# First pair of an attention and rational-MLP kernel: order of its loads, transposes and splits, and the matmul order of four MLP units

## The chip, the cores and the metric

The kernel runs on one core of one Trainium2 chip. The metric is the device time of one execution in microseconds (us); the figure for a kernel is the median of several executions. The profile is one further execution, taken by the hardware profiler; its times count from the first instruction (the span's start). Engines: PE is TensorE (matmuls; PEld are its weight loads), ACT is ScalarE, DVE is VectorE, POOL is GpSimd, SP is SyncE, which here only issues transfers. A name with q (SPq, ACTq) is the engine's queue of instructions, where transfers are issued.

## The reference

All inputs are float32 after the draw. There are 4 batches of 12 heads, 448 positions and 64 dimensions a head, then an MLP over 1792 tokens with 768 inputs and 2048 hidden units:

```
scores = (q @ k.T) / sqrt(64)
scores = cap * tanh(scores / cap)
attn   = softmax(scores)            # exp(scores - max) / (sum + 1e-9)
x      = heads side by side of (attn @ v)
h = x @ w_in
P = a[0] + a[1]*h + a[2]*h*h + a[3]*h*h*h
Q = 1 + |b[0]|*|h| + |b[1]|*h*h
out = (P / (Q + 1e-6)) @ w_out
```

## The kernel before, in words

**Attention** goes by pairs of heads p = 0 to 23. K and Q of a pair are transposed on PE (`prep_k`: three transposes of 128 columns and one of K's last 64 positions for both heads; `prep_q`: four of 112), and each is split into a high part in the matmul's number format and a low rest: kh (L350), kl (L351), qh (L378 on ACT for pair 0, L381 on DVE for the others), ql (L384). A tile (p, n) is 128 keys of pair p against its 448 queries: six matmuls (L429), kl·qh, kh·ql and kh·qh for each of two heads, into one of three PSUM buffers ps of two banks; tile (p, 3) of an odd pair holds the 64 leftover keys of two pairs in twelve matmuls. ACT takes the tile by tanh (L440) and, with cap as scale, exp (L457). DVE adds up the exps of tiles 0, 1 and 2 (L463). PE multiplies them by V (L511, L528) and sums (L594, L556).

**Order.** `Plan` keeps a list of operations with estimated costs and due times and writes out, at build time, one fixed order for every engine; on the chip each engine works its list strictly in that order and waits on semaphores. `past` gives the plan the time at which a load of the first ring is taken to have landed. `visits(p)` says in which order a pair's steps are handed to the plan; for pair 0 it is tile 0, tile 1, transposes and splits of pair 1, tile 2, and four idle matmuls (`fill`, L405), which write zeros into the first ps buffer to keep PE working. `busy` (L398) does the same around the first transposes, by the counts in WARM2.

**First loads.** Ahead of the branch on cap (the bounded body runs when |cap| is at most 40, as here) the first four heads are loaded by twelve transfers. I name them by head: K0 to K3 (384 positions, 96 KB each), T0 to T3 (K's last 64 positions, 16 KB each), Q0 to Q3 (112 KB each). Pair 0 needs heads 0 and 1, pair 1 heads 2 and 3. Before, SP issues K0, K1, T0, then K2, K3, T2, T3, Q2, Q3, and ACT issues cap (to all 128 partitions), T1, Q0, Q1. The transfers of the two queues SP and ACT use eight semaphores (DMAHW0 to 7 in the order below) in turn, so the ninth transfer is issued only when the one that had its semaphore first has landed, and what is behind it in its queue waits as well. After six warm matmuls (L1292) every engine reads cap, branches, and begins the body; `preload_act_table_set` loads the table for tanh and exp (L655).

**PSUM.** prep of pairs 0 and 1 uses the banks mi (K) and pv (Q), of pair 2 mi, and of pair 3 both banks of the third ps buffer (ps_129 in the order before, ps_133 in the order of the change). So tile (2, 2), which is written there, waits until DVE has read pair 3's transposes.

**MLP.** A unit is 128 hidden units for 896 tokens: stage1 is 36 matmuls for h into a ps buffer, of 512 and of 384 tokens (two banks); `rational` takes it through ACT and DVE (L889 to L902); `stage2` (L928) multiplies by w_out, and L955 empties its PSUM. The first four units run by L858, six matmuls for each of six input blocks, alternating between the two banks; all later units run by L843, in two blocks of 18, one a bank.

Of the kernel before, what the change touches and what calls it, by code (L numbers as in the profile page):

```python
# [13 lines left out]
I32 = mybir.dt.int32  # L14
# [32 lines left out]
WARM2 = (2, 1, 3)  # L47
# [25 lines left out]
class Plan:  # L73
# [7 lines left out]
    def __init__(self):  # L81
        self.ops = []
        self.wr, self.rd = {}, {}
        self.n = 0
        self.free = [4500.0, 4600.0, 3700.0, 3700.0, 9900.0]
        self.dma_free = 11000.0
        self.where, self.over = {}, {}
# [160 lines left out]
class Body:  # L248
# [82 lines left out]

    def prep_k(self, p):
# [61 lines left out]
    def busy(self, p, n):  # L394

        z = self.io["arena_r"][:, 0:512]
        for _ in range(WARM2[n] if p == 0 else 0):
            self.op(PE, 213, lambda: self.nc.tensor.matmul(self.PS[2][:, 1], z[:, 0:128], z, start=True, stop=True),  # L398
                    [], [("ps", 2), "turn"])
# [15 lines left out]
    def scores(self, p, n):  # L415
# [16 lines left out]
        self.op(PE, SC_NS * len(sets) + TURN_NS * first, run, [k for name, _ in sets for k in K(name)], w, early=E_SC)  # L432
# [208 lines left out]
    def attention(self):  # L641
# [11 lines left out]
        self.prep_k(0)  # L653
        self.prep_q(0)
        self.op(ACT, 1290, lambda: nc.scalar.preload_act_table_set("exp_and_others"), [], ["table"])  # L655
# [19 lines left out]
        def visits(p):  # L675
# [10 lines left out]
            if p == 0:  # L686
                return [s0, s1, (k, 1), (q, 1), s2, (self.fill, FILL[0])]
# [137 lines left out]
    def stage1(self, u, between=None):  # L825
# [384 lines left out]
    def run(self):  # L1210
        tc = self.tc
        self.rslot, self.made, self.later = {}, set(), {}
        with ExitStack() as ctx:
# [31 lines left out]
def attention_rational_mlp(ctx: ExitStack, tc: tile.TileContext, q, k, v, cap, moe_w_in, moe_w_out,  # L1245
# [4 lines left out]
    with tc.manual_schedule():  # L1250
# [15 lines left out]
        nc.scalar.dma_start(acap, cap.partition_broadcast(128))  # L1266
# [13 lines left out]
        nc.gpsimd.dma_start(a, moe_a.partition_broadcast(128))  # L1280
        nc.vector.tensor_scalar(acap.bitcast(I32), acap.bitcast(I32), 0x7FFFFFFF, None, ALU.bitwise_and)
# [11 lines left out]
        rv = nc.values_load(acap.bitcast(I32)[0:1, 0:1])  # L1293
# [40 lines left out]
```

## Time and profile before

| what | us |
|---|---|
| median of 3 runs (lowest, highest) | 659.59 (659.20, 659.76) |
| the profiled execution, its own time | 659.91 |
| its span, first to last instruction | 657.9 |
| PE busy in the span | 647.8 (98%) |
| DVE busy | 541.9 (82%) |
| ACT busy | 442.2 (67%) |

Busy shares are means over stages with different limits: attention runs to about 181 us, the MLP from there to the end. A row of the timeline gives start, duration, engine, line, operation, out<-in, shapes and count; the brackets give the idle time just ahead of it and what ended it. Neighbouring instructions of one kind are merged into a row.

### The profile page before, as it was taken

How to read it: one execution, taken by the hardware profiler on the slowest of the kernel's cores; microseconds unless marked ns; L12 is line 12 of the kernel's file. 1: busy time of each engine (PE TensorE's matmuls, PEld its weight loads, DVE VectorE, ACT ScalarE, POOL GpSimd, SP SyncE). 2: the span in 40 equal slices, each digit the busy share in tenths (PEclk: the TensorE clock that was granted, in tenths of full speed). 3: DMA queues.
4: the chain of work that ended last, by engine and by line, in shares of the span. 5: the costliest groups of instructions: out<-in, count | busy, mean ns of one | idle time of the engine just before them, and what ended most of it. 6: DMA issues, size and time to landing. Idle time of an engine off the chain costs nothing.

```text
span 657.9 us, 9767 instructions
## 1 busy us (share of the span) xinstructions
PE 647.8 (98%) x3820; PEld 542.0 (82%) x3820; DVE 541.9 (82%) x662; ACT 442.2 (67%) x531; POOL 85.0 (13%) x141
## 2 busy tenths in 40 slices
PE   8999999999999999999999999999999999999996
PEld 5555555655478899999999999999999999999996
DVE  4789899899679987977987897899699789969653
ACT  5899999999857867875457466646646565663560
POOL 4013222321200000020012002101200210120030
PEclk9999999999999999999999999999999999999999
DMA  7757864943230332195158118614821671481086
GB/s 170 186 138 171 203 163 100 199 119 85 59 86 22 128 141 92 51 197 113 48 106 158 49 49 152 158 43 86 166 68 49 128 142 60 95 170 33 1 139 203
DMA packets 79095, 74.45 MB, mean 113 GB/s; under 512 B 48456, under 2 KB 67264, under 8 KB 79040
## 3 DMA queue, kind: packets, MB, share of 16 engines
q1 hardware_dynamic: 68240, 48.68, 25.7%
q0 software_dynamic: 9648, 24.80, 22.5%
q8 instruction: 32, 0.52, 0.3%
q10 hardware_dynamic: 1152, 0.25, 0.2%
q14 instruction: 23, 0.19, 0.1%
HBM read 47.98 MB, written 25.65 MB: 112 GB/s over the span
## 4 chain that ended last, share of the span: by engine, by line
PE 82%; DVE 6%; ACT 4%; DMA 3%; issue 3%; POOL 0%; SPq 0%; DVEq 0%; POOLq 0%; ACTq 0%
PE ps L843 31%; PE ps L928 17%; PE mi L928 9%; PE pv L928 9%; PE ps L429 6%; PE mi L511 3%; DMA arena_r<-dn 2%; ACT etiles L440 2%; PE mi L594 1%; PE pv L511 1%; ACT etiles L457 1%; PE pv L528 1%; PE ps L343 1%; DMA dn<-arena_f 1%; PE ps L366 1%
## 5 line engine op out<-in xcount | busy, mean ns | idle before, releaser
L843 PE MATMUL ps<-arena_r,ring 128*128 128x512 f32 (+1 forms) x924 | 207.6, 363 | 0.0
L843 PEld LDWEIGHTS ps<-arena_r,ring 128*128 128x128 f32 x924 | 167.7, 188 | 17.5
L295 POOL DMA_DIRECT2D out_dram<-arena_f x49 | 42.0, 863 | 423.6 <-ACT arena_f L955 423.6
L928 PE MATMUL ps<-arena_r,etiles 128*128 128x384 f32 x462 | 89.7, 335 | 0.6 <-ACT arena_f L955 0.5
L457 ACT ACTIVATE etiles<-etiles,acap 128x896 f32<-128x896 f32 x84 | 85.5, 1053 | 0.2
L440 ACT ACTIVATE etiles<-ps 128x896 f32<-128x896 f32 x84 | 74.7, 921 | 13.9 <-PE ps L429 13.7
L928 PEld LDWEIGHTS ps<-arena_r,etiles 128*128 128x128 f32 x462 | 80.8, 188 | 1.3 <-ACT arena_f L955 0.8
L928 PE MATMUL mi<-arena_r,etiles 128*128 128x384 f32 x231 | 77.2, 336 | 0.0
L928 PE MATMUL pv<-arena_r,etiles 128*128 128x384 f32 x231 | 77.0, 335 | 0.0
L429 PEld LDWEIGHTS ps<-arena_r 64*128 64x128 f32 x576 | 51.0, 184 | 25.2 <-ACT etiles L457 7.8
L889 ACT ACTIVATE arena_f<-ps,b 128x896 f32<-128x896 f32 x32 | 32.3, 1009 | 54.8 <-PE ps L843 54.7
L429 PE MATMUL ps<-arena_r 64*128 64x448 f32 x576 | 67.7, 376 | 1.2 <-DVE arena_r L384 0.9
L789 ACT ACTIVATE arena_f<-arena_f 128x768 f32<-128x768 f32 x32 | 29.4, 918 | 44.1 <-DMA arena_f<-in_moe_w_out_dram 31.0
L901 ACT CAST etiles<-arena_f 128x896 fp32r<-128x896 f32 x32 | 30.3, 946 | 42.0 <-DVE arena_f L900 42.0
L893 DVE SCALAR_TENSOR_TENSOR arena_f<-arena_f,bab 128x896 f32<-128x896 f32 x32 | 36.8, 1150 | 23.8 <-ACT arena_f L890 23.8
L898 DVE SCALAR_TENSOR_TENSOR arena_f<-arena_f,one 128x896 f32<-128x896 f32 x32 | 36.7, 1148 | 11.3 <-ACT arena_f L896 11.3
L928 PEld LDWEIGHTS pv<-arena_r,etiles 128*128 128x128 f32 x231 | 43.3, 188 | 0.6
L928 PEld LDWEIGHTS mi<-arena_r,etiles 128*128 128x128 f32 x231 | 43.3, 188 | 0.6
L928 PE MATMUL ps<-ring,etiles 128*128 128x384 f32 x210 | 42.0, 334 | 0.0
L902 DVE TENSOR_TENSOR etiles<-arena_f,etiles 128x896 fp32r<-128x896 f32 x32 | 34.9, 1089 | 7.0 <-ACT etiles L901 6.8
L891 ACT ACTIVATE arena_f<-ps,a 128x896 f32<-128x896 f32 x32 | 35.3, 1104 | 3.5 <-DVE arena_f L899 3.5
L897 DVE SCALAR_TENSOR_TENSOR arena_f<-arena_f,a,ps 128x896 f32<-128x896 f32 x32 | 36.6, 1144 | 0.4
(145 smaller groups left out, 1124.2 us busy)
## 6 DMA issues: line engine op xcount, KB each, us to landing
out_dram<-arena_f POOLq DMA_DIRECT2D x49, 384.0 KB, 6.2
arena_f<-in_moe_w_out_dram SPq DMA_DIRECT2D x16, 768.0 KB, 4.3
arena_f<-in_moe_w_in_dram SPq DMA_DIRECT2D x16, 768.0 KB, 4.8
out_dram<-arena_f SPq DMA_DIRECT2D x13, 384.0 KB, 2.5
ring<-in_q_dram SPq DMA_DIRECT2D x44, 112.0 KB, 3.6
arena_r<-dn POOLq DMA_DIRECT2D x20, 224.0 KB, 5.3
ring<-in_k_dram SPq DMA_DIRECT2D x33, 128.0 KB, 3.1
ring<-in_v_dram SPq DMA_DIRECT2D x11, 384.0 KB, 3.7
```

The lines of the kernel that those rows point to most:

```text
L295: self.op(eng, (625 if local else 450) if eng == SP else 1050, lambda: e.dma_start(out, in_, **accum), r, w, nbytes=nbytes, **kw)
L429: m = nc.tensor.matmul(self.PS[i][:, j, 0:448], st[r], mv[r], start=y == 0, stop=y == len(ops) - 1)
L440: self.op(ACT, act_ns(896, True), lambda: nc.scalar.activation(e, ps, AF.Tanh), pk + ["table"], [ek], early=E_TANH)
L457: self.op(ACT, act_ns(size, sk[0][0] == "ps", 1), lambda: nc.scalar.activation(e, src, AF.Exp, scale=acap), sk + ["table"], [ek])
L843: r = nc.tensor.matmul(po[:, ts], w[:, y, kc], mv, start=kc == 0 and z == 0, stop=kc == KC - 1 and z == 2)
L889: self.op(ACT, act_ns(n, True, 1), lambda: T.activation(Bt, h, AF.Abs, scale=b[:, 0:1]), hk, bk)
L891: self.op(ACT, act_ns(n, True, 2), lambda: T.activation(A, h, AF.Identity, scale=a[:, 3:4], bias=a[:, 2:3]), hk, ak)
L893: self.op(DVE, dve_ns(n, 1), lambda: stt(Bt, C, bab[:, 1:2], Bt, ALU.mult, ALU.add), ck + ["bab"], bk)
L897: self.op(DVE, dve_ns(n, 1), lambda: stt(A, A, a[:, 1:2], h, ALU.add, ALU.mult), hk, ak)
L898: self.op(DVE, dve_ns(n, 1), lambda: stt(Bt, Bt, one, C, ALU.add, ALU.mult), ck, bk)
L902: self.op(DVE, dve_ns(n), lambda: V.tensor_tensor(GL(), A, f32(GH()), ALU.subtract), ak + K("gh", ig), K("gl", ig))
L928: r = nc.tensor.matmul(po[n][:, 0:384], st, mv[:, 384 * n:384 * n + 384], start=(y == 0 and x == 0), stop=(y == self.NCH - 1 and x == 2))
```

## The change

What it does, in the order of the program:

- cap is loaded twice: one number by ACT's queue (cap1), which decides the branch, and the 128-partition copy by POOL's queue, from which c1 and the exp's scale come.
- The twelve loads are dealt out anew: SP issues Q0, K0, T0, T1, K2, K3, T2, T3; ACT issues cap1, Q1, K1, Q2, Q3, and then loads the table, ahead of the branch.
- `prep_first` replaces prep for pair 0: Q is transposed first, into pv, then K into the third ps buffer; qh and ql are made in two halves of 224 queries, kh and kl for the first 128 keys and then for the other 384. Two `busy` matmuls (L398) are left of six.
- Tile (0, 0) runs in the order kh·qh, kh·ql, kl·qh. Pair 0 is handed to the plan as tile 0, transposes and splits of pair 1, tile 1, tile 2.
- The plan's assumed landing times and engine start times are changed.
- In the four L858 units each six matmuls go as three into one bank and three into the other.

```diff
-WARM2 = (2, 1, 3)
+WARM2 = (1, 1, 3)
...
-        self.free = [4500.0, 4600.0, 3700.0, 3700.0, 9900.0]
+        self.free = [4300.0, 4200.0, 3700.0, 3700.0, 9900.0]
...
+    def prep_first(self):
+        nc = self.nc
+        idn, c1 = self.c["ident"], self.c["c1"]
+        raw = self.io["ring"][ring_of(0)]
+        name, (S, QL) = self.qset(0)
+        K = lambda s: (name, s)
+        (pk, bk), (pq, bq) = (self.PS[2][:, 0], ("ps", 2)), (self.PV, "pv")
...
+        self.busy(0, 0)
+        self.op(PE, 390, tq, rq, [bq, "turn"])
+        self.op(PE, 440, tk, rk[:3], [bk, "turn"])
+        self.op(PE, 110, lambda: nc.tensor.transpose(pk[:, 384:512], raw["kt"][:, 0], idn), rk[3:], [bk + ("2",), "turn"])
+        self.busy(0, 1)
+        for x, s in enumerate(("qh", "qh2")):
+            t = slice(224 * x, 224 * x + 224)
+            self.op(ACT, act_ns(224, True, 1),
+                    lambda t=t: nc.scalar.activation(S[:, 2, t], pq[:, t], AF.Identity, scale=c1), [bq], [K(s)], early=E_PR)
...
+        high(slice(0, 128), "")
+        for x, s in enumerate(("", "2")):
+            t = slice(224 * x, 224 * x + 224)
+            self.op(DVE, dve_ns(224, 1),
+                    lambda t=t: nc.vector.scalar_tensor_tensor(QL[:, t], pq[:, t], c1, f32(S[:, 2, t]), ALU.mult, ALU.subtract),
+                    [bq, K("qh" + s)], [K("ql" + s)], early=E_PR)
+        low(slice(0, 128), "")
+        for f in (high, low):
+            f(slice(128, 512), "2")
...
+            if p + n == 0:
+                ops = ops[2], ops[1], ops[0]
...
-        self.prep_k(0)
-        self.prep_q(0)
-        self.op(ACT, 1290, lambda: nc.scalar.preload_act_table_set("exp_and_others"), [], ["table"])
+        self.prep_first()
+        self.plan.past("table", 4000.0)
...
-                return [s0, s1, (k, 1), (q, 1), s2, (self.fill, FILL[0])]
+                return [s0, (k, 1), (q, 1), s1, s2, (self.fill, FILL[0])]
...
-                for z, (y, mv) in enumerate(((0, h), (0, lo), (1, h))):
-                    for ts, x in zip(parts, mv):
-                        r = nc.tensor.matmul(po[:, ts], w[:, y, kc], x,
+                for ts, *x in zip(parts, h, lo, h):
+                    for z, y in enumerate((0, 0, 1)):
+                        r = nc.tensor.matmul(po[:, ts], w[:, y, kc], x[z],
                                              start=kc == 0 and z == 0, stop=kc == KC - 1 and z == 2)
...
-        nc.scalar.dma_start(acap, cap.partition_broadcast(128))
+        cap1 = T("cap1", [1, 1])
+        nc.scalar.dma_start(cap1, cap.partition_broadcast(1))
+        nc.gpsimd.dma_start(acap, cap.partition_broadcast(128))
...
-        for n in (0, 1, 2):
+        for n in (4, 0, 2, 3, 6, 7, 8, 9):
             nc.sync.dma_start(*first[n][1:3])
-        for n in (3, 4, 5):
+        for n in (5, 1, 10, 11):
             nc.scalar.dma_start(*first[n][1:3])
-        for n in (6, 7, 8, 9, 10, 11):
-            nc.sync.dma_start(*first[n][1:3])
+        nc.scalar.preload_act_table_set("exp_and_others")
...
-        rv = nc.values_load(acap.bitcast(I32)[0:1, 0:1])
+        rv = nc.values_load(cap1.bitcast(I32)[0:1, 0:1])
```

Where it moves instructions, the two orders stand below (a wait is named where an instruction has one).

SP's queue at the start, before (K0 and K1 in the first row; then T0, K2, K3, T2, T3, Q2, Q3):

```order
L1271 DMA arena_f<-in_k_dram 128x3x64 x2
L1271 DMA arena_f<-in_k_dram 64x64 [waits Pool_49]
L1275 DMA arena_f<-in_k_dram 128x3x64
L1275 DMA arena_f<-in_k_dram 128x3x64 [waits DMAHW0_49]
L1275 DMA arena_f<-in_k_dram 64x64 [waits DMAHW1_49]
L1275 DMA arena_f<-in_k_dram 64x64 [waits DMAHW2_49]
L1275 DMA arena_f<-in_q_dram 112x4x64 [waits DMAHW3_49]
```

SP's queue at the start in the change (Q0, K0, T0, T1, K2, K3, T2, T3, V):

```order
L1326 DMA arena_f<-in_q_dram 112x4x64
L1326 DMA arena_f<-in_k_dram 128x3x64
L1326 DMA arena_f<-in_k_dram 64x64 [waits Pool_49]
L1326 DMA arena_f<-in_k_dram 64x64
L1326 DMA arena_f<-in_k_dram 128x3x64 [waits DMAHW0_49]
L1326 DMA arena_f<-in_k_dram 128x3x64 [waits DMAHW2_49]
L1326 DMA arena_f<-in_k_dram 64x64 [waits DMAHW3_49]
L1326 DMA arena_f<-in_k_dram 64x64 [waits DMAHW4_49]
L1330 DMA arena_f<-in_v_dram 128x4x192 [waits DMAHW5_49]
```

T3 was the seventh load of SP and is now the eighth; its semaphore is the one of K1 (DMAHW4), T2's that of K0 (DMAHW3), K3's that of Q1 (DMAHW2).

PE from the branch to the tiles of pair 0, before (L343, L345: transposes of K; L366: of Q; L429: tiles):

```order
L343 MATMUL mi<-ident,arena_f 128x128 x3
L345 MATMUL mi<-ident,arena_f 128x128
L398 MATMUL ps_129<-arena_r 128x512
L366 MATMUL pv<-ident,arena_f 128x112 x4
L398 MATMUL ps_129<-arena_r 128x512 x3
L429 MATMUL ps_127<-arena_r 128x448 x6
L429 MATMUL ps_128<-arena_r 128x448 x6
```

The same stretch in the change (L344, L350, L356: transposes of Q, K and K's last positions for pair 0; L392, L394, L415: for pair 1; L483: tiles):

```order
L344 MATMUL pv<-ident,arena_f 128x112 x4
L350 MATMUL ps_133<-ident,arena_f 128x128 x3
L356 MATMUL ps_133<-ident,arena_f 128x128
L447 MATMUL ps_133<-arena_r 128x512
L483 MATMUL ps_131<-arena_r 128x448 x6
L392 MATMUL mi<-ident,arena_f 128x128 x3
L394 MATMUL mi<-ident,arena_f 128x128
L415 MATMUL pv<-ident,arena_f 128x112 x4
L483 MATMUL ps_132<-arena_r 128x448 x6
```

The second tile now stands behind the eight transposes of pair 1, which stood behind it before.

DVE at the preparation of pairs 2 and 3, before:

```order
L350 CAST arena_r<-mi 128x512
L351 TENSOR_TENSOR arena_r<-mi,arena_r 128x512
L381 TENSOR_SCALAR arena_r<-mi,c_61 128x448
L350 CAST arena_r<-ps_129 128x512
L384 SCALAR_TENSOR_TENSOR arena_r<-mi,c_61,arena_r 128x448
L351 TENSOR_TENSOR arena_r<-ps_129,arena_r 128x512
L381 TENSOR_SCALAR arena_r<-ps_129,c_61 128x448
L463 TENSOR_TENSOR arena_f<-etiles 128x896
L384 SCALAR_TENSOR_TENSOR arena_r<-ps_129,c_61,arena_r 128x448
L463 TENSOR_TENSOR arena_f<-arena_f,etiles 128x896
```

and in the change (L399, L400, L430, L433 are kh, kl, qh, ql; L517 the sums of exps):

```order
L399 CAST arena_r<-mi 128x512
L400 TENSOR_TENSOR arena_r<-mi,arena_r 128x512
L517 TENSOR_TENSOR arena_f<-etiles 128x896
L430 TENSOR_SCALAR arena_r<-mi,c_61 128x448
L399 CAST arena_r<-ps_133 128x512
L433 SCALAR_TENSOR_TENSOR arena_r<-mi,c_61,arena_r 128x448
L400 TENSOR_TENSOR arena_r<-ps_133,arena_r 128x512
L430 TENSOR_SCALAR arena_r<-ps_133,c_61 128x448
L517 TENSOR_TENSOR arena_f<-arena_f,etiles 128x896
L433 SCALAR_TENSOR_TENSOR arena_r<-ps_133,c_61,arena_r 128x448
```

Both sums of pair 1's exps moved up: the first ahead of pair 2's qh, the second ahead of pair 3's ql. On ACT, tiles (1, 0) and (1, 1) now go tanh, tanh, exp, exp, where before the exp of (1, 0) came ahead of the tanh of (1, 1). From pair 4 on all engines keep their order, but for the four MLP units on PE.

## Rows read from the trace of the kernel before

**Rows 1.** The page: chain that ended last, share of the span by engine.

```profile
PE 82%; DVE 6%; ACT 4%; DMA 3%; issue 3%; POOL 0%; SPq 0%; DVEq 0%; POOLq 0%; ACTq 0%
```

**Rows 2.** Timeline of PE, 7 to 24 us: start, us, line, out<-in, count, idle before.

```profile
7.75 1.78 PE L429 MATMUL ps<-arena_r 64*128 64x448 f32 x12 [0.26 <-DVE arena_r L351]
...
9.85 0.27 PE L345 MATMUL mi<-ident,arena_f 128*128 128x128 f32 x1
...
10.44 0.88 PE L429 MATMUL ps<-arena_r 64*128 64x448 f32 x6
11.25 1.21 PE L405 MATMUL ps<-arena_r 128*128 128x512 f32 x4
12.39 0.97 PE L429 MATMUL ps<-arena_r 64*128 64x448 f32 x6
...
14.42 0.86 PE L429 MATMUL ps<-arena_r 64*128 64x448 f32 x6
...
21.58 1.49 PE L429 MATMUL ps<-arena_r 64*128 64x448 f32 x12
23.47 0.88 PE L429 MATMUL ps<-arena_r 64*128 64x448 f32 x6 [0.40 <-DVE arena_r L384]
```

**Rows 3.** Timeline of DVE, 19 to 25 us.

```profile
19.35 0.69 DVE L350 CAST arena_r<-ps 128x512 fp32r<-128x512 f32 x1 [0.21 <-PE ps L366]
...
21.74 1.08 DVE L463 TENSOR_TENSOR arena_f<-etiles 128x896 f32<-128x896 f32 x1
22.74 0.68 DVE L384 SCALAR_TENSOR_TENSOR arena_r<-ps,c,arena_r 128x448 fp32r<-128x448 f32 x1
23.33 1.08 DVE L463 TENSOR_TENSOR arena_f<-arena_f,etiles 128x896 f32<-128x896 f32 x1
```

**Rows 4.** Timeline of ACT, 4 to 23 us.

```profile
4.13 1.28 ACT L655 ACT_TABLE_LOAD   x1 [4.13 <-DVE eb L1286]
...
8.96 1.73 ACT L440 ACTIVATE etiles<-ps 128x896 f32<-128x896 f32 x2 [1.51 <-PE ps L429]
10.57 1.98 ACT L457 ACTIVATE etiles<-etiles,acap 128x896 f32<-128x896 f32 x2
...
22.50 1.73 ACT L440 ACTIVATE etiles<-ps 128x896 f32<-128x896 f32 x2 [0.97 <-PE ps L429]
```

**Rows 5.** Timeline: issue of first loads by ACT's queue and by SP's.

```profile
1.73 1.18 ACTq L1273 DMA_DIRECT2D arena_f<-in_q_dram  x2
...
2.81 2.56 SPq L1275 DMA_DIRECT2D arena_f<-in_k_dram  x4
```

**Rows 6.** Transfers issued at 0.75 (K0), around 1.5 to 1.9 (K1, V), at 4.78 (T3): KB, us to landing.

```profile
arena_f<-in_k_dram SPq DMA_DIRECT2D x1, 96.0 KB, 2.9
...
arena_f<-in_k_dram SPq DMA_DIRECT2D x1, 96.0 KB, 3.6
arena_f<-in_v_dram POOLq DMA_DIRECT2D x1, 32.0 KB, 3.2
...
arena_f<-in_k_dram SPq DMA_DIRECT2D x1, 16.0 KB, 2.9
```

**Rows 7.** MLP: timeline of PE around units 0 to 5; busy time by engine, 200 to 220.

```profile
185.86 18.03 PE L858 MATMUL ps<-arena_r,ring 128*128 128x512 f32 x86
...
219.73 2.38 PE L928 MATMUL ps<-arena_r,etiles 128*128 128x384 f32 x12 [0.53 <-ACT arena_f L955]
...
230.25 3.28 PE L843 MATMUL ps<-arena_r,ring 128*128 128x384 f32 x18
...
237.53 4.28 PE L843 MATMUL ps<-arena_r,ring 128*128 128x512 f32 x18
...
200.00:220.00 20.00, 19.38 (x96) 17.00 (x96) 19.99 (x22) 15.77 (x19) 0.00 (x0) 1.00 0.13 40
```

**Rows 8.** The six warm matmuls; PE, PEld, DVE, ACT, POOL busy and granted clock, 7 to 8.

```profile
1.46 2.93 PE L1292 MATMUL w<-arena_r 128*128 128x512 f32 x6 [1.46 <-DVE arena_r L1264]
...
7.00:8.00 1.00, 0.74 (x5) 0.26 (x3) 1.00 (x2) 0.45 (x1) 0.66 (x5) 1.00 1.06 222
```

More of the change, by code (lines that the diff above doesn't have):

```diff
@@ L330, in mm, with tq, tk, high @@
         return len(ops) * (n / 2.4 + 3), run
+    def prep_first(self):
[5 more added lines that the diff above has]
+        (pk, bk), (pq, bq) = (self.PS[2][:, 0], ("ps", 2)), (self.PV, "pv")
+        rk, rq = (self.raw_keys(0, n) for n in ("rk", "rq"))
+        def tq():
+            for c in range(4):
+                r = nc.tensor.transpose(pq[:, 112 * c:112 * c + 112], raw["q"][:, c, 0:2].rearrange("p j d -> p (j d)"),
+                                        idn[0:112, 0:112])
+            return r
+        def tk():
+            for c in range(3):
+                r = nc.tensor.transpose(pk[:, 128 * c:128 * c + 128], raw["k"][:, c, 0:2].rearrange("p j d -> p (j d)"), idn)
+            return r
+        self.busy(0, 0)
[7 more added lines that the diff above has]
+                    lambda t=t: nc.scalar.activation(S[:, 2, t], pq[:, t], AF.Identity, scale=c1), [bq], [K(s)], early=E_PR)
+        def high(t, s):
+            self.op(DVE, dve_ns(t.stop - t.start), lambda: nc.vector.tensor_copy(S[:, 1, t], pk[:, t]), [bk, bk + (s,)], [K("kh" + s)], early=E_PR)
+        def low(t, s):
+            self.op(DVE, dve_ns(t.stop - t.start),
+                    lambda: nc.vector.tensor_tensor(S[:, 0, t], pk[:, t], f32(S[:, 1, t]), ALU.subtract),
+                    [bk, bk + (s,), K("kh" + s)], [K("kl" + s)], early=E_PR)
+        high(slice(0, 128), "")
[7 more added lines that the diff above has]
+            f(slice(128, 512), "2")
     def prep_k(self, p):
@@ L398, in busy @@
             self.op(PE, 213, lambda: self.nc.tensor.matmul(self.PS[2][:, 1], z[:, 0:128], z, start=True, stop=True),
-                    [], [("ps", 2), "turn"])
+                    [], [("psb", 2), "turn"])
     def fill(self, n):
@@ L419, in scores @@
         w = [("ps", i), ("psb", i), ("scores", p, n), "turn"]
+        parts = ("", "2")[:n + 1]
         K = lambda name: [(name, s) for s in ("kl", "kh", "qh", "ql")]
+        split = [(self.qset(0)[0], s + x) for s in ("kl", "kh", "qh", "ql") for x in ("2",)
+                 if s[0] == "q" and x == "2" or s[0] == "k" and x in parts] * (p == 0 or (p, n) == (1, 3))
         sets = [self.qset(p - x) for x in ((1, 0) if n == 3 else (0,))]
@@ L431, in scores @@
         first = n == 0 or p % 2 and n == 2
-        self.op(PE, SC_NS * len(sets) + TURN_NS * first, run, [k for name, _ in sets for k in K(name)], w, early=E_SC)
+        self.op(PE, SC_NS * len(sets) + TURN_NS * first, run, [k for name, _ in sets for k in K(name)] + split, w, early=E_SC)
     def softmax(self, p, n):
@@ L1232, in run @@
             self.memory()
-            for key, nk, ts in (("rk", 5, (4600.0, 8000.0)), ("rq", 4, (5000.0, 9000.0))):
+            for key, nk, ts in (("rk", 5, (3700.0, 6000.0)), ("rq", 4, (3500.0, 6200.0))):
                 for x in range(2):
                     for c in range(nk):
-                        self.plan.past((key, ring_of(0), x, c), ts[x])
+                        self.plan.past((key, ring_of(0), x, c), ts[x] + 700.0 * (c > 2 and key == "rk"))
             self.plan.past(("rv", ring_of(0), 0), 11000.0)
@@ L1280, in attention_rational_mlp @@
         nc.gpsimd.dma_start(a, moe_a.partition_broadcast(128))
+        nc.vector.tensor_scalar(cap1.bitcast(I32), cap1.bitcast(I32), 0x7FFFFFFF, None, ALU.bitwise_and)
         nc.vector.tensor_scalar(acap.bitcast(I32), acap.bitcast(I32), 0x7FFFFFFF, None, ALU.bitwise_and)
```

## The prediction

> **What bounds the kernel now.** I read the chain of waits first. It lies on PE for 82% of the span [rows 1], so an edit pays only if PE comes earlier to the next place at which it has to wait. I then looked for those places near the edits, in the timelines. At the start PE waits for the first splits, begins tile (0, 0) at 7.75 and is then held by them once more [rows 2]; ACT takes that tile at 8.96 after 1.51 us of idleness [rows 4]. From there ACT is busy without a gap until 22.50, where it waits 0.97 for PE [rows 4]. PE in turn is held at 23.47, for 0.40, by DVE's last split of pair 3 at 22.74, since tile (2, 2) is written where pair 3's transposes lie [rows 2, 3]. After 23.47 PE paces the kernel for a while. So **23.47 is the gate**: what the start gains must still be there at this row, or the rest of the kernel does not see it. In the MLP the four edited units run up to 214, but PE next waits 0.53 for ACT's L955 before 219.73, and DVE is busy for 19.99 of the 20 us from 200 to 220 [rows 7].
>
> **The change part by part.**
>
> *Own transfer of cap, table load, fewer idle matmuls.* The branch could come earlier with a smaller transfer, but PE's first matmul of the body stands behind the six warm matmuls, which end at 1.46 + 2.93 = 4.39 [rows 8]; I take nothing. The 128-partition copy goes by POOL; the nearest POOL load landed 3.2 after its issue [rows 6], so from about 0.75 it lands near 4.0, c1 is ready by 4.6, and its first use is after Q's transposes at about 5.7: covered. The table load (1.28 [rows 4]) now stands behind ACT's issue of Q3, which waits for Q0's semaphore. K0 as first load landed 2.9 after 0.75 [rows 6]; Q0 is a sixth larger, so about 3.8; with Q3's issue of 0.6 [rows 5] the table is in by 5.7, when qh is due. Nothing, up to 0.3 late.
>
> *First tile.* Q is transposed at about 5.0 to 5.6 and qh follows at 5.9 in two halves; K's splits for 128 keys are short. ql, DVE's last large piece, is ready near 7.3 and kl for 128 keys near 7.6, against 8.2 before, since tile (0, 0) was held until 8.25 or so [rows 2]. I estimate the first tanh at 8.1 in place of 8.96 [rows 4], a gain of 0.85 on this tile (0.4 to 1.1). The 128- and 224-wide splits have no row; by the 512- and 448-wide ones (0.69, 0.68 [rows 3]) they are bounded above, and I take 0.3 and 0.45.
>
> *Second tile.* It now stands behind pair 1's eight transposes on PE, so behind the landing of T3. T3 waits for K1's semaphore, and T2 ahead of it for K0's. K1 is third on ACT as Q0 was, so issued at about 1.73 [rows 5]; K1 took 3.6 before [rows 6], now with two Q loads and K0 ahead of it: I take 5.5. T2 goes at about 5.2 and takes 0.64 (2.56 for four [rows 5]), T3 follows at 5.9 and lands 2.8 to 2.9 later [rows 6]: **8.7**. Bounds: without any semaphore wait, as eighth of SP, 0.75 + 7 x 0.64 = 5.2, landing at 8.0; with K1 at 5.7 and 0.6 more for queueing, 9.1. From T3's landing: 0.15 to its transpose, then 0.59 to the next tile (9.85 to 10.44 [rows 2]), so tile (0, 1) starts at 9.45. By then kh and kl for the other 384 keys (about 8.6) are ready.
>
> *From there to the gate.* Before, PE went from tile (0, 2) at 10.44 to tile (1, 1) at 14.42, 3.98 with two rounds of fill [rows 2]. Tile (0, 1) ahead adds 0.61 (1.49 for two tiles less 0.88 for one), and 0.09 goes, because pair 1's ql no longer holds up tile (1, 0) (0.97 against 0.88 [rows 2]). So (1, 1) starts at 9.45 + 0.61 + 3.98 - 0.09 = 13.95, **0.47 earlier**. Its scores are ready 0.92 later (21.58 to ACT's 22.50 [rows 2, 4]), at 14.87, and ACT is free for it by then. Here the moved DVE order bites. The sum of pair 1's exps (L463) now stands ahead of pair 2's qh, and waits for the exp of (1, 1), the second of tanh, tanh, exp, exp. Two tanh take 1.73 and the two exps end at 10.57 + 1.98 = 12.55, 1.86 after the tanhs [rows 4]. So tanh (1, 1) ends at 14.87 + 0.92 = 15.79 and its exp at 17.65. L463 takes 1.00 before the next can start (21.74 to 22.74), qh a step of 0.60 (four steps from 19.35 to 21.74 [rows 3]). Pair 3's first split then starts at 17.65 + 1.00 + 0.60 = **19.25, against 19.35**. After it come the same four steps, one L463 and the ql as before (then the first sum of pair 1, now the second). So the gate opens at 23.37 instead of 23.47. PE arrives there 0.47 earlier and waits longer. **Gain 0.1.** Its ends: T3 at 9.1 makes it a loss of 0.3; T3 at 8.0 would give 0.8, but ACT, continuous from 8.1 on, reaches tanh (1, 1) no earlier than 14.3, which caps the gain at about 0.65. What is late next in that case is again PE, behind the gate.
>
> Three of the moved loads rest on this. By the Trainium skill (DMA: Bandwidth & Descriptors, "Issuing engines are not separate DMA queues") transfers started by different engines run on the same 16 DMA engines and interleave, so a second queue saves issue time only. No row here shows two large streams of equal size on both queues; by that rule the second half of the loads lands no earlier for having moved, which is the sum above and not the better bound.
>
> *Runs of three in the MLP.* 86 alternating matmuls took 18.03, about 0.208 each; blocks of 18 took 3.28 and 4.28, less a drain of some 0.17 each 7.22 for 36, 0.201 each [rows 7]. At most 144 x 0.007 = 1.0; with the bank changed two times in six instead of every time, 0.6. PE would only reach 219 earlier and wait 1.1 instead of 0.53: DVE and ACT, whose order here is unchanged, release it [rows 7]. **Nothing** (0 to 0.6; no reason for a loss).
>
> Sum: 659.91 of the profiled execution less 0.1; it stood 0.3 above the median. On the median, **659.5**.
>
> **The rivals.**
>
> *The start's gain is carried whole.* T3 lands near 8.0, or the gate is passed because the exp of (1, 1) is in time. For it: SP's own loads before were spaced by issue alone (0.64 each [rows 5]). Against it: two semaphores that land after 5. Gain 0.65 to 0.85: 658.8.
>
> *The MLP's runs pay.* If the wait at 219.73 were PE's own doing, 0.6 more comes off: 658.9; together with the rival above 658.2. Against it: DVE's 19.99 of 20 [rows 7].
>
> *PE's clock falls.* Slower than before. The warm matmuls went 0.43 apart, which for 512 columns is 1.2 GHz; the fills at 11.25 took 1.21 for four, 0.24 apart, 2.4 GHz [rows 2, 8]; between, PE was at work for most of the time, 0.74 of the us from 7 to 8 at a granted clock of 1.00 [rows 8]. Now four of the six idle matmuls are gone, and PE has little to do from 5 to 9.4: transposes, one tile, and waits for K1, the splits and T3. If the clock is down to 1.2 GHz when tile (0, 1) starts, the three tiles ahead of (1, 1) (nine pairs of matmuls, 0.19 more each) and eight fills (0.19 each) cost 3.2; with the clock back halfway, 1.6, and nothing ahead of the gate takes that up: 661.1. It decides if PE's work from 5 to 9.4 is too thin. The Trainium skill (TensorE: Matmul & The Clock Gate, "Part 4: PE-mode transpose") says that transposes do not engage the full clock as matmuls do; the trace before has transposes between idle matmuls at full clock, and none with so little beside them.
>
> *The change does not do what it says* (the first tanh stays near 8.96 because K1, T1 or the table is late): the second tile then moves little too, as T3 sets it: 659.6, inside the forecast.
>
> **How the numbers follow.** Forecast (gate open within 0.4 of before) 0.62; gain carried 0.24; MLP's runs pay 0.06 (with both, 0.03 of it); clock 0.08. About 0.2%, 1.3 us, is what a measurement of this kernel can tell from no change. Faster by more than that needs both gains, 0.04; slower needs the clock or a worse T3, 0.07; the same, 0.89. The forecast's own range is 659.1 to 660.0. For 8 in 10 I go to the carried gain, 658.7, and above to T3's bad end with half of a lesser clock loss, 660.2.
>
> **What would show it.** In the timeline: first tanh near 8.1; T3 landing near 8.7 and tile (0, 1) at 9.4; L517 (the sum) ahead of pair 2's qh ending near 18.7 after a wait for ACT; tile (2, 2) at 23.3 to 23.5 with PE idle for 0.7 or more before it; 138 matmuls of the four units at about 0.203 each and a wait of over 1 us ahead of L928 at 219. If tile (2, 2) starts before 22.9, the gate was not one and the first rival holds; if fills are 0.43 apart after 9, the third.

## The result and the profile after

| | kernel before | changed kernel |
|---|---|---|
| median of 6 runs beside each other (lowest, highest) | 659.74 (659.20, 661.17) | 664.49 (662.61, 665.85) |
| ratio, with its 95% interval | | 1.0068 (1.0053 to 1.0083) |
| the profiled execution, its own time | 659.91 | 665.66 |
| its span | 657.9 | 663.8 |

The change is slower by 4.75 us; the forecast was 659.5 with a range up to 660.2. The chain of waits still lies on PE, for a little more of the span than in [rows 1]:

```profile
PE 84%; DVE 6%; ACT 5%; DMA 2%; issue 2%; POOL 0%; SPq 0%; DVEq 0%; ACTq 0%; POOLq 0%
```

The start in the timeline of PE (start, duration, engine, line; L344, L350, L356 and L392, L394, L415 are transposes, L447 and L454 idle matmuls, L483 tiles), to be laid beside [rows 2]:

```profile
4.54 0.77 PE L447 MATMUL ps<-arena_r 128*128 128x512 f32 x1
5.11 0.95 PE L344 MATMUL pv<-ident,arena_f 112*128 112x112 f32 x4
...
7.06 0.78 PE L447 MATMUL ps<-arena_r 128*128 128x512 f32 x1
8.31 1.74 PE L483 MATMUL ps<-arena_r 64*128 64x448 f32 x6 [0.48 <-DVE arena_r L364]
9.98 0.90 PE L392 MATMUL mi<-ident,arena_f 128*128 128x128 f32 x3
...
11.77 2.38 PE L483 MATMUL ps<-arena_r 64*128 64x448 f32 x12
14.09 1.21 PE L454 MATMUL ps<-arena_r 128*128 128x512 f32 x4
...
24.33 1.49 PE L483 MATMUL ps<-arena_r 64*128 64x448 f32 x12
26.59 0.88 PE L483 MATMUL ps<-arena_r 64*128 64x448 f32 x6 [0.77 <-DVE arena_r L433]
```

Up to 14 us everything PE does takes longer: twelve matmuls of two tiles 2.38, where twelve of the same shape take 1.49 at 24.33; one idle matmul alone 0.78. The four fills at 14.09 take 1.21, as before. So in this execution PE was at the lower of its two levels (1.2 GHz) to about 14 us. This is read from durations, because the clock column can't be used there: the trace's clock record begins only with the rise, at 13.76 here and at 4.88 before, and ahead of it the column reads 1.00 even where the warm matmuls went 0.43 apart. Experiment 11 has a stretch that is recorded at 0.50, and three transposes of L392 take the same 0.90 there. Tile (2, 2), the gate, starts at 26.59 instead of 23.47: 3.12 late.

The MLP, in the timelines of PE and, last row, of ACT (to be laid beside [rows 7]; L911, L981, L896, L942 are the L858, L928, L843, L889 of before):

```profile
189.13 17.65 PE L911 MATMUL ps<-arena_r,ring 128*128 128x512 f32 x85
...
222.59 2.35 PE L981 MATMUL ps<-arena_r,etiles 128*128 128x384 f32 x12 [0.55 <-ACT arena_f L1008]
...
233.14 3.28 PE L896 MATMUL ps<-arena_r,ring 128*128 128x384 f32 x18
...
240.42 4.36 PE L896 MATMUL ps<-arena_r,ring 128*128 128x512 f32 x18
...
619.23 1.01 ACT L942 ACTIVATE arena_f<-ps,b 128x896 f32<-128x896 f32 x1 [4.10 <-PE ps L896]
```

The same ACT instruction before, and PE waits for nothing in between in either kernel that would explain a difference:

```profile
613.87 1.01 ACT L889 ACTIVATE arena_f<-ps,b 128x896 f32<-128x896 f32 x1 [4.06 <-PE ps L843]
```

The delay is 2.86 at 219.73 [rows 7] against 222.59, 2.89 at the block of 237.53 against 240.42, and 5.36 at 613.87 against 619.23. So the loss of this execution has **two places**: 3.1 us in the first 26, and 2.5 us that grow evenly from 240 on, in matmuls whose order the change does not touch. A block of 18 matmuls of 512 columns takes 4.36 instead of 4.28; one of 384 columns takes 3.28 as before. There are 28 units of that kind. From its start to PE's next, a 512-column matmul of theirs takes 232.7 ns on average instead of 228.9 (504 matmuls), which makes 1.9; most of the rest lies in the 384-column matmuls of L981, 174.5 ns instead of 174.0 (1341 of them, 0.7).

### The profile page after: what moved, and what is told of

It reads as the page before. It is cut to its first block, busy times and chain, and to the rows that moved or that the text cites. A ratio compares the mean times of both kernels' runs of the same rounds, so it can differ in the third digit from the quotient of the medians.

```text
span 663.8 us, 9762 instructions
## 1 busy us (share of the span) xinstructions
PE 652.7 (98%) x3816; PEld 544.7 (82%) x3816; DVE 542.4 (82%) x666; ACT 442.5 (67%) x532; POOL 85.8 (13%) x142
## 4 chain that ended last, share of the span: by engine, by line
PE 84%; DVE 6%; ACT 5%; DMA 2%; issue 2%; POOL 0%; SPq 0%; DVEq 0%; ACTq 0%; POOLq 0%
PE ps L896 31%; PE ps L981 17%; PE mi L981 9%; PE pv L981 9%; PE ps L483 6%; PE mi L565 4%; PE pv L565 2%; ACT etiles L511 2%; ACT etiles L494 2%; PE mi L648 1%; PE pv L582 1%; PE ps L392 1%; PE ps L415 1%; DMA arena_r<-dn 1%; DVE arena_f L681 1%
## 5 line engine op out<-in xcount | busy, mean ns | idle before, releaser
L896 PE MATMUL ps<-arena_r,ring 128*128 128x512 f32 (+1 forms) x924 | 209.4, 366 | 0.0
L896 PEld LDWEIGHTS ps<-arena_r,ring 128*128 128x128 f32 x924 | 167.7, 188 | 18.9
L981 PE MATMUL ps<-arena_r,etiles 128*128 128x384 f32 x462 | 90.0, 337 | 0.6 <-ACT arena_f L1008 0.6
L981 PEld LDWEIGHTS ps<-arena_r,etiles 128*128 128x128 f32 x462 | 81.0, 188 | 1.2 <-ACT arena_f L1008 0.9
L981 PE MATMUL pv<-arena_r,etiles 128*128 128x384 f32 x231 | 77.4, 336 | 0.0
L981 PE MATMUL mi<-arena_r,etiles 128*128 128x384 f32 x231 | 77.4, 336 | 0.0
L483 PEld LDWEIGHTS ps<-arena_r 64*128 64x128 f32 x576 | 52.0, 188 | 26.1 <-ACT etiles L511 7.4
L483 PE MATMUL ps<-arena_r 64*128 64x448 f32 x576 | 69.3, 382 | 1.7 <-DVE arena_r L433 1.2
L942 ACT ACTIVATE arena_f<-ps,b 128x896 f32<-128x896 f32 x32 | 32.2, 1007 | 54.0 <-PE ps L896 53.8
L981 PEld LDWEIGHTS pv<-arena_r,etiles 128*128 128x128 f32 x231 | 43.4, 188 | 0.7
L981 PEld LDWEIGHTS mi<-arena_r,etiles 128*128 128x128 f32 x231 | 43.4, 188 | 0.7
L981 PE MATMUL ps<-ring,etiles 128*128 128x384 f32 x210 | 42.3, 336 | 0.0
L955 DVE TENSOR_TENSOR etiles<-arena_f,etiles 128x896 fp32r<-128x896 f32 x32 | 34.8, 1088 | 7.4 <-ACT etiles L954 7.1
L981 PEld LDWEIGHTS ps<-ring,etiles 128*128 128x128 f32 x210 | 37.1, 188 | 0.0
```

The source lines that it names most:

```text
L483: m = nc.tensor.matmul(self.PS[i][:, j, 0:448], st[r], mv[r], start=y == 0, stop=y == len(ops) - 1)
L896: r = nc.tensor.matmul(po[:, ts], w[:, y, kc], mv, start=kc == 0 and z == 0, stop=kc == KC - 1 and z == 2)
L942: self.op(ACT, act_ns(n, True, 1), lambda: T.activation(Bt, h, AF.Abs, scale=b[:, 0:1]), hk, bk)
L955: self.op(DVE, dve_ns(n), lambda: V.tensor_tensor(GL(), A, f32(GH()), ALU.subtract), ak + K("gh", ig), K("gl", ig))
L981: r = nc.tensor.matmul(po[n][:, 0:384], st, mv[:, 384 * n:384 * n + 384], start=(y == 0 and x == 0), stop=(y == self.NCH - 1 and x == 2))
```

## The experiments

Two theories stood at the outset. For the even drift: the change declares a new tile, cap1, behind arena_r, and each tile takes a multiple of 32 bytes per partition; etiles, extra and both rings, declared later, lie 32 bytes higher (as the program is built; no trace prints an address). For the start: PE's clock, against the loads and the new order.

### 1. The shift alone, in the kernel before

```diff
         first = load_group(io, 0)
+        T("pad", [1, 1])
```

> The kernel before with one unused tile declared where the change declares cap1, so that etiles, extra and both rings lie 32 bytes higher; no instruction is added, moved or taken away. Theory A (the steady drift after 240 us in the changed kernel's trace, 2.97 us in the profiled execution, comes from where these tiles lie): 661.5 to 662.7, with the 384-column matmuls of L928 at 174 ns or more from one to the next after 260 us instead of 173.3. Rival B (the drift comes from the changed orders, or from the chip): 659.7, within 0.4 of before, 173.3 ns. The start (tile (2,2) at 23.47) is the same by both.

Measured: 663.15 against 659.66, ratio 1.0046 (1.0028 to 1.0064). An unused tile of four bytes costs 3.5 us, more than the 1.8 to 3.0 that the expectation by theory A comes to. In the timeline of PE, and of ACT in the last row:

```profile
230.89 3.28 PE L843 MATMUL ps<-arena_r,ring 128*128 128x384 f32 x18
...
238.17 4.36 PE L843 MATMUL ps<-arena_r,ring 128*128 128x512 f32 x18
...
617.42 1.01 ACT L889 ACTIVATE arena_f<-ps,b 128x896 f32<-128x896 f32 x1 [4.10 <-PE ps L843]
```

The 512-column blocks take 4.36 as in the changed kernel, and the delay grows from 0.64 at 238.17 to 3.55 at 617.42. The 0.64 stems from the start: the clock rose at 6.98, and tile (2, 2) starts at 24.12, which was expected unchanged; experiment 9, without any shift, has 6.78 and 24.02. Theory A, that the place of the tiles does it, holds.

### 2. The change without the shift

```diff
-        a, b, bab = T("a", [128, 4]), T("b", [128, 2]), T("bab", [128, 2])
+        a5, b, bab = T("a", [128, 5]), T("b", [128, 2]), T("bab", [128, 2])
+        a, cap1 = a5[:, 0:4], a5[0:1, 4:5]
...
-        cap1 = T("cap1", [1, 1])
```

> The changed kernel with cap1 in the unused part of the tile of a, so that all other tiles lie where they lay before. Theory A (place of the tiles): the drift after 240 us goes, 664.5 becomes 662.4 to 662.7, what is left is the start's 2.8 to 3.1, and the runs scatter less. Rival B: 664.5, drift of 2 to 3 us still there. Tile (2,2) at 26.6 by both.

Measured: 659.38 against 659.66, ratio 0.9999 (0.9985 to 1.0014). The expectation of 662.4 was a miss: not only the drift went but the start's loss too. PE and, in the rows so marked, DVE and ACT:

```profile
5.10 0.59 PE L344 MATMUL pv<-ident,arena_f 112*128 112x112 f32 x4
...
8.14 0.68 PE L483 MATMUL ps<-arena_r 64*128 64x448 f32 x4 [0.15 <-DVE arena_r L375]
8.74 0.55 PE L392 MATMUL mi<-ident,arena_f 128*128 128x128 f32 x3
...
9.72 1.49 PE L483 MATMUL ps<-arena_r 64*128 64x448 f32 x12
...
14.18 0.87 PE L483 MATMUL ps<-arena_r 64*128 64x448 f32 x6
...
23.62 0.87 PE L483 MATMUL ps<-arena_r 64*128 64x448 f32 x6 [0.78 <-DVE arena_r L433]
```

```profile
7.08 0.29 DVE L364 CAST arena_r<-ps 128x128 fp32r<-128x128 f32 x1 [1.34 <-PE ps L447]
...
8.00 0.28 DVE L368 TENSOR_TENSOR arena_r<-ps,arena_r 128x128 fp32r<-128x128 f32 x1
...
17.91 1.09 DVE L517 TENSOR_TENSOR arena_f<-etiles 128x896 f32<-128x896 f32 x1 [0.81 <-ACT etiles L511]
...
19.51 0.68 DVE L399 CAST arena_r<-ps 128x512 fp32r<-128x512 f32 x1
```

```profile
8.86 0.92 ACT L494 ACTIVATE etiles<-ps 128x896 f32<-128x896 f32 x1 [2.34 <-PE ps L483]
```

```profile
185.46 17.63 PE L911 MATMUL ps<-arena_r,ring 128*128 128x512 f32 x85
...
218.99 2.35 PE L981 MATMUL ps<-arena_r,etiles 128*128 128x384 f32 x12 [0.56 <-ACT arena_f L1008]
...
236.77 4.28 PE L896 MATMUL ps<-arena_r,ring 128*128 128x512 f32 x18
```

With the same instructions as the change, PE is fast here from the transposes on (four of Q in 0.59, not 0.95), and the blocks take 4.28 again.

### 3 and 4. One idle matmul more, one fewer

The first of the three counts of idle matmuls, in the changed kernel and in the kernel before:

```diff
-WARM2 = (1, 1, 3)
+WARM2 = (2, 1, 3)
```

> The changed kernel with two idle matmuls instead of one behind the branch, ahead of Q's transposes. Theory C (TensorE stays at its slower level up to 13.8 us in the changed kernel because too little matmul work follows the warm matmuls): the level rises near 4.9 us as before, transposes of Q 0.11 apart instead of 0.18, first tile's matmuls twice as close, tile (2,2) near 23.5, and 664.5 becomes 661.4 to 662. Rival D (the later landings of K0, K1, T0 and T1 and the order of pair 0 cost the time themselves, and the clock follows from the waits): tile (0,0) still near 8.0 to 8.3, tile (1,1) at 16.5 or later, 664 or more.

```diff
-WARM2 = (2, 1, 3)
+WARM2 = (1, 1, 3)
```

> The kernel before with one idle matmul instead of two behind the branch and nothing else changed: loads, order and places as before. Theory C (clock): the level does not rise near 4.9 us, tile (1,1) starts 1.5 to 3 us later than 14.42, and 659.7 becomes 661.2 to 662.7. Rival D (loads and order): K's transposes wait for their loads anyway, 659.5 to 659.9.

Measured: the change with one more 662.95 (ratio 1.0045, 1.0028 to 1.0061), still with the shift and its 4.36:

```profile
238.90 4.36 PE L896 MATMUL ps<-arena_r,ring 128*128 128x512 f32 x18
```

It was expected at 661.4 to 662. Before with one fewer 659.36 (0.9999, 0.9988 to 1.001). In its profile the clock rose late, at 7.40, and tile (2, 2) starts at 24.01; but in the kernel before that happens with both idle matmuls too (experiment 9), and the median shows nothing. So the missing idle matmul does not by itself cost the kernel before anything that can be told; theory C as I put it (one matmul decides) falls, and rival D too, since in experiment 2 the loads and orders of the change cost nothing either.

### 5 to 7. Which distance counts

Twice the distance; arena_r moved along with the others; the rings alone (each against the kernel before):

```diff
         first = load_group(io, 0)
+        T("pad", [1, 16])
```

> The kernel before with etiles, extra and both rings 64 bytes higher instead of 32; nothing else. Theory A1 (what counts is whether these tiles begin at a multiple of 64 bytes, as they do after the shift by 32, or 32 beside one, as before): as before, 659.4 to 660, 512-column matmuls of L843 at 229 ns from one to the next, no drift after 240 us. Rival A2 (any move away from the old place costs): about 663, 232 to 233 ns.

```diff
+        T("pad", [1, 1])
         io["arena_r"] = T("arena_r", [128, ARENA_R], F32R)
```

> The kernel before with arena_r moved up by 32 bytes too, so that the tiles from which weights and moving data are read keep their distances and only their place changes. Theory A3 (place of weights against moving data counts): 659.4 to 660, 229 ns. Rival A4 (each tile's own place counts): 663 or more, 512-column matmuls at 232 to 233 ns or slower.

```diff
+            T("pad", [1, 1])
             self.io["ring"][0:2] = [ring_views(self.ringtile(n, F32)) for n in range(2)]
```

> The kernel before with only the two rings 32 bytes higher; arena_r, etiles and extra as before. L843 takes its weights from a ring, L928 from etiles; L843's moving data come from arena_r and extra, L928's from arena_r and ring. If the place of the weights counts: L843 at 232 to 233 ns for 512 columns as with all tiles moved, L928 with data from arena_r at 173.3 as before, time 661.5 to 662.5. If the place of the moving data counts: L843 at 229.5 as before, only L928 with data from a ring slower, time 659.5 to 660.

One row of PE each, from the timelines of the three in this order:

```profile
237.27 4.35 PE L843 MATMUL ps<-arena_r,ring 128*128 128x512 f32 x18
```

```profile
237.47 4.28 PE L843 MATMUL ps<-arena_r,ring 128*128 128x512 f32 x18
```

```profile
237.41 4.36 PE L843 MATMUL ps<-arena_r,ring 128*128 128x512 f32 x18
```

The delay against the kernel before, taken at this block and at the ACT instruction of 613.87 as above:

| kernel | what lies elsewhere | block of 18 | delay grows by | median, before beside it |
|---|---|---|---|---|
| changed | etiles, extra, rings by 32 | 4.36 | 2.47 | 664.49, 659.74 |
| 1 | the same, nothing else | 4.36 | 2.91 | 663.15, 659.66 |
| 2 | nothing | 4.28 | -0.01 | 659.38, 659.66 |
| 3 | as changed | 4.36 | 2.47 | 662.95, 659.66 |
| 5 | by 64 | 4.35 | 2.37 | 661.96, 659.23 |
| 6 | arena_r and all behind it by 32 | 4.28 | 0.62 | 660.28, 659.23 |
| 7 | rings by 32 | 4.36 | 2.61 | 662.60, 659.23 |

Experiment 6 settles that it is the **distance** between arena_r and the tiles behind it, not where a tile begins: all of them moved together, the matmuls of L843 run as before. (Its 0.62 is a single step at 524, where an L928 waits 0.15 for ACT's L955 and the next few run late, no drift; the median's 1.05 more, ratio 1.0012 with 1.0001 to 1.0023, is near what can be told.) Experiment 5 takes away the simple rule that multiples of 64 bytes are equal. Experiment 7 shows that for L843 it is the place of the rings against arena_r. It was expected to leave alone the L928 that read arena_r and etiles; but the L928 into pv that do so, with both their tiles where they were, took 176 ns on average to PE's next start (225 matmuls) instead of 174. And in experiment 1 the 512-column matmuls that stream from extra slowed as well, from 226.7 to 231.1 ns (42 matmuls), though extra and rings kept their distance. So which accesses meet is not settled.

### 8. The change once more

> The changed kernel once more, unchanged, beside the others. If the clock's late rise (13.8 us) belongs to the program, it is there again and the median is 664 or more. If it is the luck of one execution, TensorE's level rises between 5 and 8 us this time, tile (2,2) starts at 23.5 to 24.5, the drift after 240 us is 2.9 to 3.0 as before, and the median lies at 662.5 to 664.

Measured: 663.06 against 659.23, ratio 1.0080 (1.0049 to 1.0111); the medians alone give 1.0058. Four of its six runs lie between 661.90 and 663.49, two at 667.6. The profiled one took 663.49. PE:

```profile
4.99 0.55 PE L344 MATMUL pv<-ident,arena_f 112*128 112x112 f32 x4
...
23.81 0.88 PE L483 MATMUL ps<-arena_r 64*128 64x448 f32 x6 [0.77 <-DVE arena_r L433]
...
74.49 2.09 PE L483 MATMUL ps<-arena_r 64*128 64x448 f32 x18 [1.69 <-DVE arena_r L433]
...
238.64 4.36 PE L896 MATMUL ps<-arena_r,ring 128*128 128x512 f32 x18
```

It is the same program, and this time PE is fast from 5 us on: the gate opens at 23.81 instead of 26.59. The 2.8 us between the two executions are TensorE's clock, and not a property of the change that every execution has. The drift is there again (1.11 at 238.64, 3.58 at the ACT instruction, which stands at 617.45). The wait of 1.69 at 74.49 (0.25 before, at 72.69) goes back to a transfer through DRAM on which DVE waits 4.17 at 70.42; experiment 9, without any shift, has a wait of 1.48 at the same tile, so it belongs to neither cause.

### 9. The MLP's runs of three alone

In the kernel before, only L854 to L860 as in the change:

```diff
-                for z, (y, mv) in enumerate(((0, h), (0, lo), (1, h))):
-                    for ts, x in zip(parts, mv):
-                        r = nc.tensor.matmul(po[:, ts], w[:, y, kc], x,
+                for ts, *x in zip(parts, h, lo, h):
+                    for z, y in enumerate((0, 0, 1)):
+                        r = nc.tensor.matmul(po[:, ts], w[:, y, kc], x[z],
```

> The kernel before with only the four MLP units in runs of three; start, loads and places as before. Theory M (the rival that the MLP's runs pay, in part): PE goes from L858's start to L928 in 28.24 instead of 28.61 (0.37 less, as with the whole change without the shift) and the wait ahead of L928 at 219 stays 0.5 to 0.6, so all of it reaches the end: about 0.4 less than before. Forecast's step (swallowed at 219): the wait grows to 0.9 and the time stays within 0.1 of before.

```profile
186.99 17.63 PE L858 MATMUL ps<-arena_r,ring 128*128 128x512 f32 x85
...
215.23 1.20 PE L928 MATMUL ps<-arena_r,etiles 128*128 128x384 f32 x6
...
220.41 2.35 PE L928 MATMUL ps<-arena_r,etiles 128*128 128x384 f32 x12 [0.54 <-ACT arena_f L955]
```

From 186.99 to L928 at 215.23 are 28.24; before it was 28.61, from 185.86 [rows 7] to this row:

```profile
214.47 1.21 PE L928 MATMUL ps<-arena_r,etiles 128*128 128x384 f32 x6
```

The wait at 220.41 is 0.54, as the 0.53 of before, and theory M reads this as a gain that is not swallowed. It is not so. The wait ends with L955, the last piece of a chain of ACT and DVE that starts where DVE has waited for a transfer through DRAM (tile dn); this is the row, before and in experiment 9:

```profile
192.19 1.16 DVE L627 TENSOR_TENSOR arena_f<-arena_r,arena_f 128x448 f32<-128x448 f32 x2 [3.50 <-DMA arena_r<-dn]
```

```profile
192.99 1.16 DVE L627 TENSOR_TENSOR arena_f<-arena_r,arena_f 128x448 f32<-128x448 f32 x2 [3.17 <-DMA arena_r<-dn]
```

From there to the end of PE's wait are 27.54 and 27.42, and in every one of the thirteen profiles L955 (L1008) starts 26.6 to 26.7 after that row. In experiment 9 the transfer landed 0.33 earlier, counted from the L858 rows at 185.86 and 186.99 (6.00 after them against 6.33), and that is most of the 0.45 by which the wait ended sooner after them (33.42 against 33.87). Experiment 4 is the comparison that decides: with the old order of the MLP and a landing at 5.98 its wait ends 33.40 after that start. So PE's 0.37 is swallowed, and in the median nothing is seen: 659.79 against 659.96, ratio 1.0001 (0.9989 to 1.0013).

### 10 and 11. Without the shift: two idle matmuls, and none

Experiment 2 with the first count of WARM2 at 2, and at 0.

> The changed kernel with cap1 in the tile of a (all tiles where they lay before) and two idle matmuls behind the branch: the candidate for a version ahead of both. By the rows of the change without the shift: 0.4 from the MLP, 0.1 to 0.4 from the start, so 658.8 to 659.3 where before gives 659.2 to 659.7. If the second idle matmul costs PE time at the start that reaches the gate, 0.2 more.

> The changed kernel with cap1 in the tile of a and no idle matmul behind the branch. If the late rise of TensorE's clock, seen in one execution, is a matter of how PE's work behind the warm matmuls falls, it comes more often with less work there: part of the runs 3 to 5 us above the others (662 to 665 beside 659), or the profiled execution with its fast matmuls only from 8 to 14 us on. If it is luck alone: the same times as with one idle matmul, 659.0 to 660.5 and one run in twelve above.

Measured, both against 659.96: with two 659.26, ratio 1.0000 (0.9985 to 1.0015); with none 660.62, ratio 1.0004 (0.9991 to 1.0018). The candidate beats neither the kernel before nor experiment 2 by anything that can be told. The profiled execution with none shows the clock in the busy times by stretch (PE, PEld, DVE, ACT, POOL, then granted clock, DMA share, GB/s):

```profile
7.00:8.00 1.00, 0.53 (x4) 0.24 (x4) 0.53 (x2) 0.00 (x0) 0.93 (x3) 1.00 0.54 78
8.00:9.00 1.00, 0.84 (x4) 0.56 (x6) 1.00 (x4) 0.00 (x0) 0.73 (x6) 0.80 0.90 288
9.00:10.00 1.00, 1.00 (x6) 0.47 (x5) 0.70 (x2) 0.34 (x1) 0.64 (x2) 0.50 0.91 226
...
11.00:12.00 1.00, 1.00 (x7) 0.68 (x7) 0.94 (x2) 0.65 (x1) 0.00 (x0) 0.50 0.93 208
12.00:13.00 1.00, 1.00 (x12) 0.70 (x8) 1.00 (x3) 0.43 (x1) 0.00 (x0) 0.99 0.90 201
```

and in PE's timeline:

```profile
4.60 0.85 PE L344 MATMUL pv<-ident,arena_f 112*128 112x112 f32 x4 [0.22 <-issue]
5.68 0.52 PE L350 MATMUL ps<-ident,arena_f 128*128 128x128 f32 x3 [0.22 <-DMA arena_f<-in_k_dram]
6.91 0.30 PE L356 MATMUL ps<-ident,arena_f 128*128 128x128 f32 x1 [0.71 <-DMA arena_f<-in_k_dram]
6.96 0.47 PE L447 MATMUL ps<-arena_r 128*128 128x512 f32 x1
7.91 0.47 PE L483 MATMUL ps<-arena_r 64*128 64x448 f32 x2 [0.47 <-DVE arena_r L364]
...
9.55 0.90 PE L392 MATMUL mi<-ident,arena_f 128*128 128x128 f32 x3
...
25.54 0.88 PE L483 MATMUL ps<-arena_r 64*128 64x448 f32 x6 [0.77 <-DVE arena_r L433]
```

The clock had risen by 5.68 (three transposes in 0.52), fell to half in the ninth microsecond, and was back in the thirteenth. What PE did ahead of the fall is in the same run: three transposes at 5.68, a wait of 0.71 for K's tail, one transpose and one idle matmul to 7.43, and a wait of 0.47 for the split. Experiments 2 and 8 have waits of 0.48 and 0.66 for K's tail and of 0.47 and 0.48 for the split at the same places, and no fall; so what sets it off is not shown. The gate stands at 25.54, 1.9 later than in experiment 2. So what my third rival describes, a clock that is down when tile (0, 1) starts, does occur; with one idle matmul the late rise came in one profiled execution of three with that order (the change's first, against experiments 2 and 8).

## Why the prediction was wrong, point by point

**The step that failed is the first, "Own transfer of cap".** It priced the new transfer, the branch and the engines that read cap, and took nothing. It did not price cap1 itself: a new tile in the middle of the allocation. That moved every tile declared behind it by 32 bytes away from arena_r, and PE reads weights from rings and etiles while it streams data from arena_r. The sum was made of instructions and waits, and no instruction's duration was allowed to change. The runs show in its place blocks of 4.36 instead of 4.28: the price is 3.5 us by experiment 1, and without the shift the change measures 659.38 by experiment 2. That this is near the 659.5 forecast for the whole shows little for the terms: the gate alone missed by 0.25, where the whole sum was a gain of 0.1, and the medians can't tell such amounts. None of the rivals had the price. The diff showed the line; and since PE is on the chain for 82% of the span [rows 1], anything that slows its matmuls by 1% costs several microseconds.

**"PE's clock falls"** was given 0.08 and priced at 1.6 to 3.2. The price fits the execution in which the clock was low (2.8 by experiment 8 against the first profile), but not by its terms: the fills, half of the 3.2, ran at the full level from 14.09 on, and the transposes and the first tile, which the sum left out, at half. The clock did not fall there either; it came up late. What I had wrong is that the program decides it. Two executions of one program stand on either side. By the Trainium skill (TensorE: Matmul & The Clock Gate, "Part 1: The HAM clock gate") the point of the rise varies from run to run, since the monitor does not start with the kernel; these traces agree, and show more than the half microsecond that it names: fast from 4.99 in one, from about 14 in the other. The rule of the Trainium skill that I cited, that transposes do not engage the full clock (same page, "Part 4: PE-mode transpose"), is not what decided: in experiment 8 the same transposes run at the full level. How much of the 4.75 this cause makes is open. The shift's 3.5 leaves 1.25, and the late rise is the candidate for it, not more: experiment 3, with one idle matmul more, gave 662.95, the change itself 664.49 and 663.06 in two sets, but which of the executions without a profile had the late rise can't be seen.

**The gate** held. In experiment 2, PE reaches tile (2, 2) early and waits 0.78 (forecast: 0.7 or more) for DVE's last split; the tile starts at 23.62 (forecast 23.37, before 23.47), and at 23.81 in experiment 8. The moved sums do what the forecast said: the first of them waits for ACT's exp until 17.91, and pair 3's first split starts at 19.51 (forecast 19.25, before 19.35). The quarter of a microsecond comes from PE: tile (1, 1) starts at 14.18, not 13.95. So the gain of 0.1 was a loss of 0.15 there, inside the ends given. No run could have told the two apart: in five runs that leave the start alone (experiments 1, 5, 6, 7 and 9) the gate opens at 23.59 to 24.12, later where the clock rose later (at 4.68 to 6.98).

**First tile: missed.** Forecast 8.1 for the first tanh, measured 8.86 in experiment 2, 0.10 ahead of 8.96 [rows 4]. The row of DVE names the releaser: kh at 7.08 waits for L447, the idle matmul behind K's last transpose, which writes the same ps buffer as the transposes. All of DVE's splits shift with it: PE waits for ql, forecast ready near 7.3, until 8.14, and kl for 128 keys, forecast ready near 7.6, starts only at 8.00. The error was not harmless: it holds tile (0, 0) on PE until 8.74, and what follows there is late by it, down to the gate.

**Second tile: the time was near, by luck.** Tile (0, 1) starts at 9.72 in experiment 2 (forecast 9.45), but T3 does not set it. By the trace's record of the transfers T3 was issued at 5.50 (forecast 5.9) and had landed at 8.18 (forecast 8.7); pair 1's transposes follow tile (0, 0) at 8.74 without a wait. The first tile's lateness stands where I had put T3's.

**The MLP's runs of three: the size was wrong, the end right.** I took 0.6 to 1.0 off PE; PE saved 0.37 (28.24 against 28.61, in experiments 2 and 9 alike; 0.2046 a matmul over 138 where 0.203 was forecast). That ACT and DVE release the wait at 219 and swallow the gain holds, by the rows of experiment 9. The sign that I named for it, a wait of over 1 us, did not come (0.54 there, 0.56 in experiment 2): I had left out that this chain hangs on a transfer through DRAM, whose landing, counted as in experiment 9, varies between 5.1 and 6.3 over the runs. In experiment 11, with 5.1, L955 was in time and PE did not wait at all.

**Range and chances.** The range was built from the terms of the sum and the rivals, all of them waits. With PE on the chain almost throughout, a term for "PE's own rate changes" had to be in it.

## What to carry to other kernels

When a change declares a tile, compare where every other tile lies before and after, and put small new data into the unused end of a tile that exists, as experiment 2 does, or behind everything else, which no run here tried. When a loss grows evenly through code that the change does not touch, compare the duration of equal blocks (here 18 matmuls, 4.28 and 4.36) before looking for waits, and undo the allocation alone. And profile the same program twice before a cause is read from its first microseconds: TensorE's clock came up at 5 us in one execution and at 14 in another.

## What the runs showed of the hardware that I had not expected

PE's pace depends on where the tiles from which it reads lie against each other. With etiles, extra and rings 32 bytes higher against arena_r, a 512-column matmul in the later units took 232.7 ns on average to PE's next start instead of 228.9 (504 each, experiment 1 against before), those of 384 columns in L843 stayed at 174; with arena_r moved along (experiment 6), the 512-column figure was 228.9 again. It is not always a loss: in the alternating units (L858) the 512-column figure went from 237.4 to 232.1 ns (68 each), so the old place is the better one for the blocks of 18, of which there are most. It also decides what an order is worth: from L858 to L928 the alternating order takes 28.61 at the old place and 28.15 at the new one (experiment 1), the runs of three 28.24 and 28.28 (experiment 2 and the change). The Trainium skill (SBUF — State Buffer, "SBUF: two separate sides") has it that on the engines' side only the port pair shared by VectorE and GpSimd causes contention, and the table of ports further down (same page, "Who interferes with whom") gives TensorE two independent read ports, one of them for weight loads. No run here shows two engines colliding in this. But TensorE's pace did change with the place of its tiles, by 3.7 ns in 229, and the measurement decides; whether its own two streams meet, or something else does, no run here shows.

TensorE's clock can also fall again after it has risen: 0.50 granted from 9 to 12 us in experiment 11, after a stretch of transposes, two waits and one idle matmul.
